# An attention and feed-forward kernel on one core: C v in 64x32 tiles, and another order of all steps

## The chip, the cores and the metric

The kernel runs on one core of a Trainium2 chip. The core has a matrix engine (TensorE, PE in the profile), three engines for vectors (VectorE = DVE, ScalarE = ACT, GpSimd = POOL), a sync engine (SP), and 16 DMA engines that all queues share. Each engine takes its own instructions strictly in the order in which they were written, and waits for the others by semaphores. The metric is the time of one execution in device microseconds (us), as the median of several runs.

## The reference

For 8 batches of 8 heads with 576 rows of 64 columns, the Nystroem form of attention, and behind it a feed-forward step on all 4608 tokens:

```
q_lm, k_lm = means of 18 rows each: 32 landmarks a head
A  = softmax(q k_lm^T / 8)        576 x 32
Bm = softmax(q_lm k_lm^T / 8)      32 x 32
C  = softmax(q_lm k^T / 8)         32 x 576
Z  = Bm^T / (|Bm|_1 |Bm|_inf);  six times  Z = 2 Z - Z Bm Z
x  = A Z C v                       576 x 64 a head, the 8 heads side by side: 4608 x 512
out = ((x w1) * (x w2)) w3 w_out   w1, w2: 512 x 1024, w3: 1024 x 1024, w_out: 1024 x 512
```

Inputs and outputs are fp32.

## The kernel before

The work is cut into steps, each the instructions of one engine, with a short name. A *quad* n (0 to 15) is four heads of one batch: batch b has the quads 2b and 2b+1. The kernel never forms x: it multiplies the small matrix W = Z C v (32 x 64 a head) by w1 and w2 first, and then A by the result.

- **Weights.** `w3n` loads w3 in eight chunks, four DMAs each on SP, `wf` loads w_out in four pieces, half on SP and half on ACT. DVE transposes a chunk (`tr`, L572), ACT and DVE split it and w_out into a high and a low fp16 half (`wh` L579, `wl` L587, `woh` L561, `wol` L566). PE multiplies chunk j with w_out in eight steps `mm{j}0` to `mm{j}7` of three products each, and ACT brings the result out (`wo`, L606). The outcome is w34 = w3 w_out in eight parts.
- **Quads.** `lq` loads k and q of a quad on POOL's queue, with a cast to fp16 (L651). DVE transposes them (`T`, L676). The means come from PE for the quads 0 and 1 (`mp`) and from POOL for the others (`ma` L684, `mb` L691); ACT scales them (`mk`). PE forms the scores of C (`S`, 32x32 tiles) and of A and Bm (`A`, whole array); maxima, exponentials, sums and norms follow on DVE, ACT and POOL (`sm`, `sw`, `sb`, `se`, `ct`, and `ar`, `am`, `as`, `ae`, `au`, `bo`, `an`, `aT`).
- **C v** (`C{b}`, `cv_mm`, L891). `lv` loads v on SP, four DMAs a quad. For each of nine chunks of 64 rows a product in a 64x64 tile takes two heads' columns of exp(C) against two heads' v: of the four blocks that this gives, the two with C and v of the same head count. A tenth product forms the sums with `unit64`. `co` (L909) divides by the sums on DVE.
- **Z.** For groups of one or two batches: `N` (norms), five rounds of `x` on PE and `y` on DVE, then `Z` and `zo`. All are fp32 products in 32x32 tiles.
- **W and U.** `W{b}` (`w_mm`) multiplies Z and C v, four products a batch; `wp` and `wq` split the result in two fp16 halves; `U` (64x32 tiles) multiplies by w1 and w2, and ACT brings U out (`uo`, L1035).
- **Dense work.** `d` multiplies U by A for both of w1 and w2, ACT copies one (`e`, L1110), DVE multiplies the two (`f`, L1116), `g` multiplies by w34, `h` (ACT, L1130) scales and `st` stores, two DMAs a tile of 128 tokens.

All matrix products are issued by the helper `mm`, so they have one line, L492; they are told apart by their tiles (xz is `x` and `Z`; vb,ecT is `C`; zb,cv is `W`; w,wT is `U`; aT,u is `d`; w,ab is `g`; wo,w3t is `mm`; bm is `N`). An fp32 product is issued as two matmuls with a weight load each.

**What sets the order.** A planner (`Plan.run`, L146) runs when the kernel is built. It keeps a ring of buffers for every kind of tile, and the eight PSUM banks as one ring. Step by step it takes, on the engine that can begin first, the ready step with the lowest entry in the table `PRIO`, with costs, DMA rates and instruction fetches that it assumes. The order that results is written out once and is fixed when the program runs. `GATE` holds loads back: the k and q of the quads 0 and 1 wait for `gw1`, a small POOL copy that reads w_out's second piece, and all later ones and the loads of w1 and w2 (`lw`, L669) wait for `gw3`, which reads its fourth. Eighteen products on a zeroed tile (`warm`, step `wu`) come first on PE.

Of the kernel before, what the change touches and what calls it, by code (L numbers as in the profile page):

```python
# [11 lines left out]
ALU = mybir.AluOpType  # L12
# [17 lines left out]
GATE = {**{n: ["gw3"] for n in range(2, 16)}, 0: ["gw1"], 1: ["gw1"], "w": ["gw3"]}  # L30
MEANPE = range(2)
WARM = 18
# [5 lines left out]

class Task:
    def __init__(self, name, eng, occ, fn, deps, acq, rel, anchor, off, kind, mode, lat, dma, n):  # L40
        self.name, self.eng, self.occ, self.fn, self.n = name, eng, occ, fn, n
        self.deps, self.acq, self.rel = deps, acq, rel
        self.anchor, self.off, self.kind = anchor, off, kind
        self.mode, self.lat, self.dma = mode, lat, dma
        self.prio = PRIO[name]
        self.ready = 0.0
        self.start = self.free = self.end = None


class Plan:  # L50
# [6 lines left out]

    LAT = {"PE": 0.2, "ACT": 0.15, "DVE": 0.13, "POOL": 0.1, "SP": 0.0}
    SELF = {"PE": 0.0, "ACT": 0.14, "DVE": 0.11, "POOL": 0.08, "SP": 0.0}
    NEAR = {"PE": 0.08, "ACT": 0.05, "DVE": 0.05, "POOL": 0.05, "SP": 0.0}  # L60
    SWITCH = 0.093
    BACK = 0.093
    FIRST, LAND = 1.3, 1.0
    PIECE, AHEAD, FETCH = 256, 60, 3.4
    STAY = 0.6
    RATE = {1: 0.88, 2: 1.08, 3: 1.08}
    BEGIN = {"PE": 1.0, "ACT": 0.7, "DVE": 0.8, "POOL": 1.2, "SP": 0.7}

    def __init__(self):
        self.tasks, self.by = [], {}  # L70
        self.rings, self.slot, self.left = {}, {}, {}
# [12 lines left out]
    def _slots(self, acq):  # L84
        got, when, taken = [], 0.0, set()
        for ring, key, uses in acq:
            free = self.rings[ring]
            some = [i for i, f in enumerate(free) if f is not None and (ring, i) not in taken]
            if not some:
                return None  # L90
            best = min(some, key=lambda i: (free[i], i))
            taken.add((ring, best))
            when = max(when, free[best])
            got.append((ring, key, best, uses))
        return when, got

    def _landed(self, limit):

        going, come = self.going, self.come
        while True:  # L100
            act = [q for q in QUEUES if going[q]]
            nxt = min([come[q][0][0] for q in QUEUES if come[q]], default=None)
            if not act and nxt is None:
                return None
            if not act:
                step = max(0.0, nxt - self.now)
            else:
                all_ = sum(going[q][0][1].dma[1] for q in act)
                rate = {q: self.RATE[len(act)] * going[q][0][1].dma[1] / all_ for q in act}
                step = min(going[q][0][0] / rate[q] for q in act)  # L110
                if nxt is not None:
                    step = min(step, max(0.0, nxt - self.now))
            if self.now + step > limit:
                step = limit - self.now
                if step <= 0.0:
                    return None
                for q in act:
                    going[q][0][0] -= step * rate[q]
                self.now = limit
                return None  # L120
            for q in act:
                going[q][0][0] -= step * rate[q]
            self.now += step
            for q in QUEUES:
                while come[q] and come[q][0][0] <= self.now + 1e-9:
                    t = come[q].pop(0)[1]
                    going[q].append([t.dma[0], t])
            for q in act:
                if going[q][0][0] <= 1e-9:
                    return going[q].pop(0)[1]  # L130

    def _finish(self, t):
        for key in t.rel:
            rec = self.left[key]
            rec[0] -= 1
            rec[1] = max(rec[1], t.end)
            if rec[0] == 0:
                self.rings[rec[2]][self.slot[key]] = rec[1]
        for u in self.after.get(t.name, ()):
            self.waiting[u.name] -= 1  # L140
            same = t.eng == u.eng and not t.dma
            u.ready = max(u.ready, t.free + self.SELF[t.eng] if same else t.end)
            if not self.waiting[u.name]:
                self.avail[u.eng].append(u)

    def run(self):  # L146
        free = dict(self.BEGIN)
        self.now, self.going, self.come = 0.0, {q: [] for q in QUEUES}, {q: [] for q in QUEUES}
        issued, landed = {q: 0 for q in QUEUES}, {q: [] for q in QUEUES}
        done, have, fetched = 0, [0.0, 0.0], 0.0  # L150
        mode = None
        self.waiting = {t.name: len(t.deps) for t in self.tasks}
        self.after, then = {}, {}
        for t in self.tasks:
            for d in t.deps:
                if d[0] == "~":
                    then.setdefault(d[1:], []).append(t)
                else:
                    self.after.setdefault(d, []).append(t)
        self.avail = avail = {e: [] for e in self.LAT}  # L160
        for t in self.tasks:
            if not self.waiting[t.name]:
                avail[t.eng].append(t)
        order, n = [], len(self.tasks)
        while len(order) < n:
            best = None
            for e, cand in avail.items():
                opts, first = [], None
                for t in cand:
                    at = max(free[e], t.ready)  # L170
                    if t.dma and issued[e] >= 8:
                        if len(landed[e]) <= issued[e] - 8:
                            continue
                        at = max(at, landed[e][issued[e] - 8])
                    if first is not None and at > first + self.NEAR[e]:
                        continue
                    got = ()
                    if t.acq:
                        found = self._slots(t.acq)
                        if found is None:  # L180
                            continue
                        at, got = max(at, found[0]), found[1]
                    if e == "PE" and mode is not None and t.mode != mode:
                        at += self.SWITCH if mode == "full" else self.BACK
                    opts.append((at, t, got))
                    if first is None or at < first:
                        first = at
                if not opts:
                    continue
                near = [o for o in opts if o[0] <= first + self.NEAR[e]]  # L190
                pick = min(near, key=lambda o: o[1].prio - (self.STAY if e == "PE" and o[1].mode == mode else 0.0))
                if best is None or pick[0] < best[0]:
                    best = pick
            t = self._landed(best[0] if best else 1e9)
            if t is not None:
                t.end = self.now + self.LAND
                landed[t.eng].append(t.end)
                self._finish(t)
                continue
            if best is None:  # L200
                left = [t.name for t in self.tasks if t.start is None]
                raise RuntimeError(f"stuck with {len(left)}: {left[:12]} {self.rings}")
            at, t, got = best
            e = t.eng
            avail[e].remove(t)
            t.start = at
            late = 0.0
            if e == "PE":
                mode = t.mode
                while (done + t.n + self.AHEAD) // self.PIECE >= len(have) - 1:  # L210
                    k = len(have) - 1
                    now = at + late + t.occ * max(0.0, self.PIECE * k - self.AHEAD - done) / t.n
                    late += max(0.0, have[k] - now)
                    fetched = max(fetched, now, have[k]) + self.FETCH
                    have.append(fetched)
                done += t.n
            t.free = free[e] = at + late + t.occ
            t.end = t.free + t.lat
            for ring, key, pick, uses in got:
                self.rings[ring][pick] = None  # L220
                self.slot[key] = pick
                self.left[key] = [uses, 0.0, ring]
            if t.dma:
# [1011 lines left out]
```

## Time and profile before

| | |
|---|---|
| median of 3 runs | 280.58 us (279.47 to 281.23) |
| the profiled execution | 280.17 us |
| its span, first to last instruction | 278.3 us |
| busy: PE | 257.2 us (92%) |
| busy: DVE | 194.0 us (70%) |
| busy: ACT | 164.0 us (59%) |
| busy: POOL | 132.3 us (48%) |
| mean granted clock of PE | 0.985 |
| HBM | 38.8 MB read, 9.4 MB written |

A busy share is a mean over the whole span. It says which engine has most to do, not what is late at a given place. Matmuls are pipelined, so a busy PE isn't one at its peak; small tiles run beside one another. The prediction therefore reads the busy times stretch by stretch, and the waits with their places. In the rows, "A <- B" at the end of a line tells what an engine waited for; "issue" is time in which it waited for nothing that the profile shows.

### The profile page before, as it was taken

How to read it: one execution, taken by the hardware profiler on the slowest of the kernel's cores; microseconds unless marked ns; L12 is line 12 of the kernel's file. 1: busy time of each engine (PE TensorE's matmuls, PEld its weight loads, DVE VectorE, ACT ScalarE, POOL GpSimd, SP SyncE). 2: the span in 40 equal slices, each digit the busy share in tenths (PEclk: the TensorE clock that was granted, in tenths of full speed). 3: DMA queues.
4: the chain of work that ended last, by engine and by line, in shares of the span. 5: the costliest groups of instructions: out<-in, count | busy, mean ns of one | idle time of the engine just before them, and what ended most of it. 6: DMA issues, size and time to landing. Idle time of an engine off the chain costs nothing.

```text
span 278.3 us, 9596 instructions
## 1 busy us (share of the span) xinstructions
PE 257.2 (92%) x3934; PEld 168.3 (60%) x3934; DVE 194.0 (70%) x470; ACT 164.0 (59%) x413; POOL 132.3 (48%) x147
## 2 busy tenths in 40 slices
PE   8668999989996699999999999899999999999993
PEld 2234344444693586667668777686687576864771
DVE  4669999999996499999999979674157153440440
ACT  0725565456446465999579543763645857648551
POOL 0362899999999398999997333003000000000000
PEclk9799999999999799999999999999999999999999
DMA  7999999999999426584958123502601043313334
GB/s 174 237 226 236 233 240 235 241 256 224 182 219 240 111 45 126 145 186 56 194 111 212 42 65 96 141 2 48 144 4 41 18 97 79 78 39 78 75 79 113
DMA packets 22509, 37.34 MB, mean 134 GB/s; under 512 B 3520, under 2 KB 7616, under 8 KB 22464
## 3 DMA queue, kind: packets, MB, share of 16 engines
q1 hardware_dynamic: 16128, 24.13, 35.5%
q0 software_dynamic: 5696, 11.54, 23.3%
q10 hardware_dynamic: 640, 1.05, 1.5%
q8 instruction: 31, 0.51, 0.8%
q14 instruction: 14, 0.11, 0.1%
HBM read 38.80 MB, written 9.44 MB: 173 GB/s over the span
## 4 chain that ended last, share of the span: by engine, by line
PE 58%; DMA 16%; POOL 10%; DVE 5%; issue 4%; ACT 4%; SPq 0%; ACTq 0%; POOLq 0%; DVEq 0%
PE bank L492 58%; DMA w3n<-in_moe_w_dram 5%; DMA nat<-in_k_dram 4%; POOL ls L691 4%; DMA ab<-in_moe_w_out_dram 3%; DMA vb<-in_v_dram 3%; POOL ls L684 3%; DMA u<-in_moe_w_out_dram 1%; POOL ah L825 1%; ACT lm L712 1%; POOL ea L797 1%; POOL nat L651 1%; DVE tiny L811 1%; DVE T L676 1%; DVE bank L572 1%
## 5 line engine op out<-in xcount | busy, mean ns | idle before, releaser
L1116 DVE TENSOR_TENSOR ab<-asb,bank 128x384 f16<-128x384 f16 x96 | 50.2, 547 | 41.1 <-ACT asb L1110 38.4
L492 PE MATMUL bank<-aT,u 128*128 128x192 f16 x768 | 70.0, 247 | 0.6 <-issue 0.5
L492 PEld LDWEIGHTS <-u 128*128 128x128 f16 x768 | 64.7, 99 | 7.4 <-issue 0.7
L492 PE MATMUL bank<-w,ab 128*128 128x512 f16 x288 | 67.3, 379 | 0.0
L1110 ACT CAST asb<-bank 128x384 f16<-128x384 f32 x96 | 45.2, 483 | 16.5 <-PE bank L492 13.2
L492 PE MATMUL bank<-wo,w3t 128*128 128x512 f16 x192 | 47.0, 388 | 3.5 <-ACT wo L561 2.2
L492 PEld LDWEIGHTS <-ab 128*128 128x128 f16 x288 | 27.2, 98 | 28.6 <-issue 1.4
L691 POOL TENSOR_TENSOR ls<-ls 128x128 f32<-128x128 f32 (+2 forms) x56 | 40.8, 729 | 3.4
L1130 ACT ACTIVATE osb<-bank 128x512 f32<-128x512 f32 x36 | 21.5, 602 | 32.4 <-PE bank L492 31.9
L1035 ACT CAST u<-bank 128x512 f16<-128x512 f32 x64 | 33.0, 616 | 5.9 <-PE bank L492 5.9
L825 POOL TENSOR_TENSOR ah<-ea,tiny 128x576 f16<-128x576 f32 x16 | 18.5, 1162 | 33.3 <-DVE aT L834 32.8
L684 POOL TENSOR_TENSOR ls<-nat 128x1152 f32<-128x1152 f16 x14 | 33.2, 2375 | 2.3 <-ACT lm L712 1.6
L492 PEld LDWEIGHTS <-w3t 128*128 128x128 f16 x192 | 18.3, 101 | 26.2 <-issue 4.9
L676 DVE STREAM_TRANSPOSE T<-nat 128x576 f32<-128x576 f32 x32 | 24.1, 755 | 2.3 <-DMA nat<-in_q_dram 1.6
L492 PE MATMUL bank<-T 32*32 32x288 f16 (+1 forms) x320 | 19.0, 293 | 4.3 <-issue 2.2
L797 POOL TENSOR_TENSOR ea<-ea,tiny 128x608 f32<-128x608 f32 x16 | 19.4, 1214 | 3.1 <-DVE tiny L791 3.1
L492 PE MATMUL bank<-xz 32*32 32x64 f32 (+1 forms) x768 | 17.0, 215 | 2.8 <-issue 2.6
L761 ACT ACTIVATE ec<-bank,tiny 128x288 f32<-128x288 f32 x32 | 16.0, 504 | 5.1 <-DVE tiny L753 5.0
L492 PE MATMUL bank<-vb,ecT 64*64 64x128 f32 x576 | 18.5, 272 | 0.2 <-issue 0.2
L492 PEld LDWEIGHTS bank<-xz 32*32 32x32 f32 x768 | 13.1, 105 | 9.0 <-issue 4.8
L492 PE MATMUL bank<-w,wT 64*32 64x512 f16 x512 | 17.3, 378 | 1.1 <-ACT ec L761 1.1
L492 PEld LDWEIGHTS bank<-vb,ecT 64*64 64x64 f32 x576 | 16.6, 133 | 1.7 <-issue 0.9
(76 smaller groups left out, 292.5 us busy)
## 6 DMA issues: line engine op xcount, KB each, us to landing
vb<-in_v_dram SPq DMA_DIRECT2D x64, 144.0 KB, 4.7
out_dram<-osb SPq DMA_DIRECT2D x72, 128.0 KB, 2.4
nat<-in_k_dram POOLq DMA_DIRECT2D x16, 288.0 KB, 7.4
nat<-in_q_dram POOLq DMA_DIRECT2D x16, 288.0 KB, 7.9
w3n<-in_moe_w_dram SPq DMA_DIRECT2D x32, 128.0 KB, 12.2
w<-in_moe_w_dram POOLq DMA_DIRECT2D x4, 512.0 KB, 16.2
u<-in_moe_w_out_dram ACTq DMA_DIRECT2D x4, 128.0 KB, 4.5
ab<-in_moe_w_out_dram ACTq DMA_DIRECT2D x4, 128.0 KB, 4.1
```

The source lines that it names most:

```text
L492: nc.tensor.matmul(out_, lhsT, rhs, start=start, stop=stop, **({} if pos is None else {"tile_position": pos}))
L572: nc.vector.transpose(out=bank(at(f"w3f{j}{h}")).rearrange("p (e g i) -> p g e i", e=4, g=4), in_=w3n[at(f"w3n{j}")].rearrange("p g (e x) ...
L676: nc.vector.transpose(out=Ts[at(f"T{n}")][:, GRP * t:GRP * t + GRP] .rearrange("p r l e -> p (r l e)").bitcast(FP32), in_=nats[at(f"nat{n} ...
L684: nc.gpsimd.tensor_tensor(out=l, in0=nat[:, :, 0:9, :], in1=nat[:, :, 9:18, :], op=ALU.add)
L691: nc.gpsimd.tensor_tensor(out=l[:, :, x:x + m, :], in0=l[:, :, x:x + m, :], in1=l[:, :, y:y + m, :], op=ALU.add)
L761: nc.scalar.activation(out=ecs[at(f"ec{n}")][:, hp, :], in_=two(f"pS{n}")[hp][:, 0:288], func=AXF.Exp, scale=SCALE, bias=t[:, 2 + hp:3 + h ...
L797: nc.gpsimd.tensor_tensor(out=ea, in0=ea, in1=tinies[at(f"ta{n}")][:, 0:19].unsqueeze(2).to_broadcast([128, 19, M]), op=ALU.subtract)
L825: nc.gpsimd.tensor_tensor(out=ahs[at(f"ah{n}")].rearrange("p g m r -> p g r m"), in0=eas[at(f"ea{n}")][:, 0:GRP, :].rearrange("p (g r) m - ...
L1035: nc.scalar.copy(out=uu[at(f"u{b}{qd}")][:, wi, 512 * half:512 * half + 512], in_=bank(at(f"pU{b}{wi}{half}{qd}")))
L1110: nc.scalar.copy(out=asb[at(f"as{b}{j}{ch}")], in_=d1_ps(b, j, ch)[0])
L1116: nc.vector.tensor_mul(abts[at(f"ab{i // 2}")][:, 2 * j:2 * j + 2, CH * (i % 2):CH * (i % 2) + CH], asb[at(f"as{b}{j}{ch}")], d1_ps(b, j, ...
L1130: nc.scalar.activation(out=osb[at(f"os{i}")], in_=bank(at(f"pE{i}")), func=AXF.Copy, scale=2.0 ** -12)
```

## The change

- **C v, each head by itself.** The products go from 64x64 to 64x32 tiles: 32 columns of one head's exp(C) against that head's 64 columns of v. There are eight products a chunk instead of four, half as wide. A batch is cut in two steps, `C{b}a` (chunks 0 to 4) and `C{b}` (chunks 5 to 8 and the sums), which may have other steps between them.
- **W in two products.** C v now stands with one head in each 32 rows, so `W` takes two products of 128 columns instead of four of 64, and `co` handles half the columns.
- **The first q and k aren't gated.** The quads 0 and 1 load without `gw1`. The first w3 chunk is loaded by SP and ACT, two DMAs each, ahead of w_out on both.
- **Warm-up** is four steps of six products, which the order places.
- **The order is given.** `PRIO` and the planner's run are gone. A list `ORDER` names every step in order, with the buffers that it takes. Each engine's steps keep the order in which the list names them.
- **The last tile** (tile 35) is formed in two halves of 256 columns, each with its own scaling and two stores, one of them on ACT's queue.

The diff, cut. The whole list `ORDER` has some 70 lines; its first lines, and those around the first dense steps, are shown.

```diff
-GATE = {**{n: ["gw3"] for n in range(2, 16)}, 0: ["gw1"], 1: ["gw1"], "w": ["gw3"]}
+GATE = {**{n: ["gw3"] for n in range(3, 16)}, 0: [], 1: [], 2: ["gw3"], "w": ["gw3"]}
-WARM = 18
+WARM = 6
+ORDER = """
+w3n0a.0 w3n0.0:0 ca w3n0a w3n0 cb lq00:0 wf0a.0 cc wf0s.0 wf0a wf0s lq01 wf1a.0 wf1s.0 lq10:1 wf1a wf1s lq11
+wf2a.0 wf2s.0 wf2s wf3s.0 tr00:0.0 wf3s zz wh00 tr01:1 wu1:2 w3n1.0:1 wh01 wu0:3 T00:0 woh0 gw0 w3n1.1 wl01 wf2a
+wl00 wu3:4 woh1 wol0 wf3a.0 w3n1.2 wf3a mm00:5 T01 mp0:6 woh2 gw1 w3n1 wol1 woh3 wol2 mm01 mk0:0 wol3 w3n2.0:2
+lt0 T10:1 A0:7.2 woh5 gw2 w3n2.1 mm02 ar0:0 woh4 S0:1.3 wol5 mm03 am0:0 w3n2.2 wol4 mp1:0 sm0:1 woh6 gw3 w3n2
+lq20:2 woh7 w3n3.0:0 T11 mm04 as0 mk1:1 w3n3.1 wol6 mm05 w3n3.2 lq21 wol7 sw0 ae0 w3n3 mm06 lq30:3 sb0 tr10:4.1
...
+S6:2.3 aT4:4 U010:7.1 am6:1 N1:6.3 uo0101 sm6:7 uo0100 mm76 se50:1 T80:0 sw6 lq101 mm77 se51 bt1 T81 as6 C1a:1.7
+mk7:1 sb6 no1:0 d000:4.5 an5:0 C1 lt7 e000:0 ct5:1 ma8:0 se60:0 aT5:5 d011:6.4 wo7 lv6.0:2 f000:0 se61 lv6.1
...
     def run(self):
...
+        order = []
+        for word in ORDER.split():
+            name, _, slots = word.partition(":")
+            t = self.by[name]
+            for (_, key, _), x in zip(t.acq, slots.split(".") if slots else ()):
+                self.slot[key] = int(x)
+            order.append(t)
...
-    def load_w3(j):
-        def fn(a):
-            nc.sync.dma_start(
+    def load_w3(j, eng, a0):
+        def fn(x):
+            a = a0 + x
+            eng.dma_start(
...
-                        r, o = slice(64 * (h2 ^ qd), 64 * (h2 ^ qd) + 64), 64 * h2
-                        if c < NC9:
-                            mm(ps[qd][o:o + 64, 0:128],
-                               ecTs[at(f"ecT{n}")][r, c, :, :].rearrange("p a m -> p (a m)"),
-                               vbs[at(f"vb{n}")][r, :, c, :],
-                               start=(c == 0), stop=(c == NC9 - 1), pos=(r.start, o))
+                        r = slice(64 * (h2 ^ qd), 64 * (h2 ^ qd) + 64)
+                        for a in range(2):
+                            o = 64 * h2 + 32 * a
+                            if c < NC9:
+                                mm(ps[qd][o:o + 32, 0:D], ecTs[at(f"ecT{n}")][r, c, a, :], vbs[at(f"vb{n}")][r, a, c, :],
+                                   start=(c == 0), stop=(c == NC9 - 1), pos=(r.start, o))
...
-            for x in range(2):
-                for s in range(2):
-                    zb = zbs[at(f"zb{i}")][:, 2 * b - 2 * GROUPS[i][0] + s, :, :]
-                    mm(ps[64 * s:64 * s + 64, 0:128].rearrange("p (e a m) -> p a e m", e=2, a=2)[:, x], cvs[at(f"cv{b}")][:, s, x, :],
-                       zb.rearrange("p (e a) m -> p a e m", a=2)[:, x], pos=(0, 64 * s))
+            for s in range(2):
+                mm(ps[64 * s:64 * s + 64, 0:128], cvs[at(f"cv{b}")][:, s, :],
+                   zbs[at(f"zb{i}")][:, 2 * b - 2 * GROUPS[i][0] + s, :, :].rearrange("p h m -> p (h m)"), pos=(0, 64 * s))
...
-        add(f"C{b}", "PE", 2.2, cv_mm(b), deps=[f"ct{n0}", f"ct{n1}", f"lv{n0}", f"lv{n1}", "cc"],
-            acq=both(f"pC{b}", 1),
+        cvd = [f"ct{n0}", f"ct{n1}", f"lv{n0}", f"lv{n1}", "cc"]
+        add(f"C{b}a", "PE", 0.85, cv_mm(b, 0, 5), deps=cvd, acq=both(f"pC{b}", 1),
+            rel=[f"ecT{n0}", f"ecT{n1}", f"vb{n0}", f"vb{n1}", f"mx{n0}", f"mx{n1}"],
+            at=(p, 2.0), mode="64x32", kind="C", n=160)
+        add(f"C{b}", "PE", 0.85, cv_mm(b, 5, 10), deps=[f"C{b}a"],
...
+            for c in range(8):
+                mm(ps[:, 0:256], ab[:, c, 256:384], w34[:, c, 256 * h:256 * h + 256], start=(c == 0), stop=(c == 7))
```

More of the change, by code (lines that the diff above doesn't have):

```diff
@@ L82, in add @@
         return t
[L84 to L144, printed above, removed]
@@ L146, in run @@
-    def run(self):
[L147 to L223, printed above, removed]
-                issued[e] += 1
-                self.come[e].append((t.free + self.FIRST, t))
-                for u in then.get(t.name, ()):
-                    self.waiting[u.name] -= 1
-                    u.ready = max(u.ready, t.free)
-                    if not self.waiting[u.name]:
-                        avail[e].append(u)
-            else:
-                self._finish(t)
-            order.append(t)
-        while True:
-            t = self._landed(1e9)
-            if t is None:
-                return order
-            t.end = self.now + self.LAND
```

205 lines of the change are left out of this document (146 added, 59 removed), and 166 rows, old and new, of the table PRIO.

## The prediction

> **What bounds the kernel now.** I read the busy time in stretches of 10 us first, then PE's waits, then the chain in order of time. (Columns of the stretches: length, busy us of PE, PEld, DVE, ACT, POOL, granted clock, DMA share, GB/s.)
>
> ```profile
> 0.00:10.00 10.00, 7.02 (x18) 2.45 (x18) 4.24 (x28) 1.87 (x3) 0.68 (x6) 1.00 0.82 197
> 10.00:20.00 10.00, 6.66 (x21) 2.34 (x21) 7.14 (x11) 4.99 (x10) 6.50 (x12) 0.83 1.08 225
> 20.00:30.00 10.00, 8.91 (x86) 5.30 (x87) 9.99 (x20) 4.41 (x15) 3.44 (x5) 1.00 1.12 235
> ...
> 80.00:90.00 10.00, 7.64 (x254) 5.38 (x253) 7.16 (x27) 5.64 (x17) 9.58 (x12) 1.00 1.03 233
> 90.00:100.00 10.00, 7.39 (x103) 6.45 (x104) 6.07 (x16) 6.08 (x19) 5.00 (x4) 0.83 0.42 90
> ...
> 270.00:280.00 10.00, 3.82 (x18) 1.56 (x16) 0.00 (x0) 1.79 (x3) 0.00 (x0) 0.85 0.34 79
> sum 280.00, PE 257.22 PEld 168.30 DVE 194.00 ACT 164.05 POOL 132.35; mean PE 9.19 PEld 6.01 DVE 6.93 ACT 5.86 POOL 4.73
> ```
>
> PE bounds it: 257.2 of 278.3 us busy. The 21.1 idle us are 7.4 in the first 30 (2.98, 3.34, 1.09), 5.0 between 80 and 100, 4.5 behind the last product, and 4.2 in all the rest. Two of these stretches also have a clock of 0.83, that is some 3.4 us at half speed, which loses 1.7 us each. So an edit pays if it takes work from PE or closes one of the two holes. The holes near 85 and 92:
>
> ```profile
> PE bank L492 <- issue: 5.9, 5, 2.6
> ...
> 84.16 2.15 issue
> 86.31 3.67 PE bank L492 x128
> 89.98 2.63 issue
> ...
> 203.12 0.51 issue
> ...
> q8 instruction: 31, 0.51, 0.8%
> ```
>
> PE waits here for no engine. The first row is PE's waits, the next ones the chain, the last one the DMA queues. PE's 7868 instructions (counted in the program) came in 31 transfers, so about 256 each, and between the two stops lie 128 products with 128 weight loads: exactly one piece. I read this as PE running out of instructions. At 86 to 92.6 a piece took 3.67 + 2.63 = 6.3 us to come, at a DMA share of 1.0; at 203 the 128 products ahead of the stop reach back to about 200.7, so there it took 2.9.
>
> **The change, part by part.** *C v.* One batch now, then what a product costs in other tiles:
>
> ```profile
> 111.22 2.19 PE L492 MATMUL bank<-vb,ecT 64*64 64x128 f32 x72
> 113.24 0.24 PE L492 MATMUL bank<-tiny,unit 64*64 64x2 f32 x8
> 113.41 0.45 PE L492 MATMUL bank<-T 32*32 32x288 f16 x16
> ...
> 121.18 0.44 PE L492 MATMUL bank<-bm 32*32 32x32 f32 x30
> ...
> 88.11 0.65 PE L492 MATMUL bank<-xz 32*32 32x64 f32 x32
> 88.69 0.94 PE L492 MATMUL bank<-w,wT 64*32 64x512 f16 x16
> ...
> L492 PE MATMUL bank<-bm 32*32 32x32 f32 x128 | 2.2, 192 | 0.3 <-issue 0.3
> L492 PE MATMUL bank<-wo,w3t 128*128 128x512 f16 x192 | 47.0, 388 | 3.5 <-ACT wo L561 2.2
> ```
>
> 80 records take 113.41 - 111.22 = 2.19 us, 27 ns each. They become 160 of half the columns in eight tiles instead of four. If columns alone count, that is half, 1.09. If starts count: 30 starts of 32 columns took 0.44 - 0.19 = 0.25, 8.3 ns each, so 1.33; and 64 fp32 columns on four tiles (32 records in 88.69 - 88.11, less 0.14 for the change of tiling below) took 14 ns, so 2.2, no gain. I take 1.33, the row where no tile is waited for twice: 8 x (2.19 - 1.33) = **-6.8** (bounds -8.8 and 0).
>
> *Changes of tiling.* In the two instruction orders PE changes its tiling 81 times before and 122 after: C v is cut in two with dense work between, and small steps are mixed more finely with dense ones.
>
> ```profile
> 49.36 2.75 PE L492 MATMUL bank<-wo,w3t 128*128 128x512 f16 x12
> 52.04 0.43 PE L492 MATMUL bank<-xz 32*32 32x64 f32 x16
> 52.40 0.93 PE L492 MATMUL bank<-wo,w3t 128*128 128x512 f16 x3
> ```
>
> Twelve products last 2.75, so with the 388 ns of one they start 0.215 apart and end their turn after 2.58; the next step starts after 2.68: 0.10 for going in. The 16 of xz take 0.36 to the next start, and another 16 (0.58 above) 0.22 more, so 0.14 for coming out. Mean 0.115: 41 x 0.115 = **+4.7** (bounds 4.1 and 5.7).
>
> *W and its scaling.* Two products of 128 columns for four of 64 stream as much, and the smaller DVE work behind C v (0.1 us a batch) runs where DVE is off the path: 0. The last tile cut in halves is no longer last in the new order, so the end (last product to the end of the span, 4.4 us) stays: 0.
>
> *The start.* The first rows of the time line:
>
> ```profile
> 1.36 7.02 PE L492 MATMUL bank<-aT 128*128 128x512 f16 x18 [1.36 <-DVE aT L510]
> 7.81 1.32 DVE L572 STREAM_TRANSPOSE bank<-w3n 128x512 f32<-128x512 f32 x2 [3.73 <-DMA u<-in_moe_w_out_dram]
> 10.58 0.40 PE L492 MATMUL bank<-wo,w3t 128*128 128x512 f16 x1 [2.20 <-ACT wo L561]
> 11.92 0.72 POOL L651 DMA_DIRECT2D nat<-in_k_dram  x1
> 14.20 0.83 POOL L612 COPY gates<-ab 128x1 f32<-128x1 f32 x2
> 17.65 0.78 DVE L676 STREAM_TRANSPOSE T<-nat 128x576 f32<-128x576 f32 x1 [0.74 <-DMA nat<-in_k_dram]
> 20.00 0.78 DVE L676 STREAM_TRANSPOSE T<-nat 128x576 f32<-128x576 f32 x1 [1.58 <-DMA nat<-in_q_dram]
> 20.71 1.28 DVE L572 STREAM_TRANSPOSE bank<-w3n 128x512 f32<-128x512 f32 x2
> 31.28 0.61 PE L492 MATMUL bank<-wo,w3t 128*128 128x512 f16 x2
> ```
>
> Now k and q are issued at 11.92, behind W_out's gate, and k is used 5.7 us later, q 2.35 after that. After, they are issued behind POOL's first constant, at about 1.4, next to two other queues, so I put the four loads at 8, 11, 14.5 and 17.5 (about 3.2 apart, not 2.35). DMA runs at 0.82 in the first 10 us and 1.08 behind them, so there is room for hardly 3 us of transfers: what k and q gain, W_out loses, and its last piece moves from 14.2 to about 18. The first w3 chunk, at the head of two queues, comes at about 6.2 instead of 7.8. DVE is in order: w3 transpose, then the memset that the warm-up products wait for, then the transpose of k (8.1), and only then the halves of w3 and W_out. So warming starts at 7.2 instead of 1.4. Its first 18 products took 7.0, mostly at half speed; I take 5.8, as the clock rises by the middle: first real product at 13.0 instead of 10.6. From 6.2 on DVE has 22 steps until the transpose of the second w3 chunk: four of q/k and eight of W_out by the rows below, ten smaller ones, 14.5 us by their durations and some 13.5 as they overlap (two transposes take 1.32 in a row above). With waits of some 2.9 for W_out and the mean that transpose comes at 22.6 instead of 20.7, but with 4.3 us of q/k work done that came later before. Down to the first product of the third w3 chunk (31.28 now) this makes 32.3: **+1.0** (bounds: -2 if DVE never waits, +3 if the warm-up is cold throughout, 18 x 0.43 = 7.7). The new order holds one more warm-up group in front of the second q/k; that is in it.
>
> ```profile
> L676 DVE STREAM_TRANSPOSE T<-nat 128x576 f32<-128x576 f32 x32 | 24.1, 755 | 2.3 <-DMA nat<-in_q_dram 1.6 <-DMA nat<-in_k_dram 0.7
> L566 DVE SCALAR_TENSOR_TENSOR wo<-u,wo 128x512 f16<-128x512 f32 x4 | 2.6, 686 | 0.0
> ```
>
> *Instructions.* 9112 instead of 7868, 36 pieces. C v is now 320 instructions in about 1.6 us, cut so that a piece's border falls inside. The holes of today close, because the dense work of batch 0 moves between C 0, C 1 and C 2: 2.15 + 2.63 + 1.7 of half speed = **-6.5**. In their place, adding up PE's work piece by piece with the durations above, the shortest pieces after hold 2.7, 2.8 (C 1, C 2), then 2.8, 2.9, 3.6 and 3.8 us. At 2.9 us a fetch they stop PE for 0.4 in all, at 6.3 the two around C 1 and C 2 and the 4.3 between them for 9.1. By then fewer loads are queued than at 84 now, so I take 4.2 there and 2.9 behind: 1.5 + 1.4 + 0.3 = **+3.2** (bounds 0.4 and 9.1).
>
> *The rest.* Two queues are passed. On SP the first two v loads now go between the w3 chunks 4 to 7; those chunks are used later and among dense work, so 0. On POOL the four W1/W2 loads move behind more q/k work:
>
> ```profile
> L684 POOL TENSOR_TENSOR ls<-nat 128x1152 f32<-128x1152 f16 x14 | 33.2, 2375 | 2.3 <-ACT lm L712 1.6 <-issue 0.7
> L691 POOL TENSOR_TENSOR ls<-ls 128x128 f32<-128x128 f32 (+2 forms) x56 | 40.8, 729 | 3.4
> L797 POOL TENSOR_TENSOR ea<-ea,tiny 128x608 f32<-128x608 f32 x16 | 19.4, 1214 | 3.1 <-DVE tiny L791 3.1
> w<-in_moe_w_dram POOLq DMA_DIRECT2D x4, 512.0 KB, 16.2
> ```
>
> Ahead of the last one POOL has four means (2.4 + 40.8/14 = 5.3 each), seven steps of 1.2, and twenty issues of 0.6, some 40 us, most of it behind 18: it is issued near 57 and lands between 65 and 73, where the first U product wants it at about 69 (12 us of PE work ahead of the first dense one). I take 0; late, it holds PE up to 3. The 4.2 idle us elsewhere I leave (DVE is as full as now until the dense work): 0 (bounds -2 and +3, W1/W2 in it).
>
> Sum: -6.8 + 4.7 + 1.0 - 6.5 + 3.2 = -4.4, so the span 278.3 becomes 273.9. The profiled run was 280.17, 1.9 above its span, and close to the median 280.58: **275.8**.
>
> A page of the Trainium skill speaks against the change. "TensorE: Matmul & The Clock Gate", section "Wait — 56ns, not 53.3ns?", says that matmul starts never come closer than about 25 ns, however narrow; by it C v would take 160 x 25 = 4.0 us a batch, and the time would be some 297. The row of bm, 30 starts in 0.25 us, does not agree: beside one another in small tiles they start at 8.3.
>
> **The rivals.**
> 1. *All covers hold.* C v at 1.09, fetches at 2.9 everywhere, DVE never late: -2.0, -2.8, -3.0, so 268. For it: the order leaves no piece under 2.7 us. Against: DMA at 1.03 in 80 to 90.
> 2. *Instructions bind, slower than before.* Place: C 1 and C 2 with the first dense work. If DMA is as full there as now, 6.3 us a piece gives 9.1 for 3.0, and half speed returns behind such a stop (1.7): 275.8 + 7.8 = 283.6. It decides from about 5.5 us a piece, where the loss (8.0) eats the gain. For it: two of the five stops now lie there. Against: part of the loads are through by then.
> 3. *C v isn't faster* (14 ns a record, as xz): +6.8, so 282.6. For it: xz has the same 64 fp32 columns. Against: xz uses four tiles, C v eight.
> 4. *A start costs what it costs now*, 27 ns: 160 x 27 = 4.3 us a batch instead of 1.33, +24, so 300. Against it: bm's row. The rule of the Trainium skill cited above is of this kind.
> 5. *A load comes late in an in-order queue.* DVE stands at k's transpose if that load lands at 11 instead of 8, or PE at the first U product for W2: +3 to +5, so 280.
>
> **How the numbers follow.** Forecast 0.45 (272 to 279), rival 1 0.2, rival 2 0.15, rival 3 0.1, rival 5 0.07, rival 4 0.03. A measurement here tells some 1%, 2.8 us. Faster: rival 1 and four fifths of the forecast, 0.57; slower: rivals 2, 4 and a little of 3, 0.2; the rest 0.23. The range of 8 in 10 goes from rival 1 to rival 2 with a margin: 267 to 285.
>
> **What would show it.** C v: 160 records a batch in 1.3 to 1.6 us. PE's waits on issue: 3 to 4 us, under 2 each, none followed by half speed. The first real product near 13, the third w3 chunk near 32. The first dense product, now in the row below, near 82. Wrong it would be if DVE or PE stand for a load before 30 us by more than 3, or if C v costs 2 us or more.
>
> ```profile
> 93.58 1.44 PE L492 MATMUL bank<-aT,u 128*128 128x192 f16 x8
> ```

## The result, and the profile after

| | before | after |
|---|---|---|
| median of 20 runs each | 278.48 us (275.68 to 282.62) | 281.38 us (278.46 to 284.39) |
| profiled run, its span | 280.17, 278.3 us | 282.35, 280.6 us |
| ratio, 95% interval | | 1.0105 (1.0081 to 1.0129) |

The kernel became 1.05% slower, where 1.7% faster was predicted; 281.38 lies inside the range of 267 to 285, but on the other side of the kernel before. Span against span it is +2.3 us instead of -4.4. Some executions of every kernel here fall into a slower state: the ratios, here and below, compare only the others, while the medians are over all.

The changed kernel in stretches of 10 us, with the columns of the prediction's table (the last row adds up thirty stretches, the last of them empty):

```profile
60.00:70.00 10.00, 7.81 (x69) 3.49 (x68) 9.93 (x25) 6.00 (x17) 9.89 (x11) 1.00 1.11 242
70.00:80.00 10.00, 9.72 (x81) 3.75 (x80) 6.45 (x15) 5.37 (x14) 8.03 (x9) 0.83 1.09 229
...
90.00:100.00 10.00, 8.06 (x260) 6.97 (x250) 7.58 (x21) 4.36 (x13) 9.61 (x11) 0.83 0.76 156
...
sum 300.00, PE 255.43 PEld 163.78 DVE 192.06 ACT 161.81 POOL 132.04; mean PE 8.51 PEld 5.46 DVE 6.40 ACT 5.39 POOL 4.40
```

PE is busy for 255.4 us instead of 257.2, so the work itself hardly shrank, and it stands idle for 25 us instead of 21. The holes of before at 84 and 92 are smaller, but there is a new one between 60 and 70, and the clock of 0.83 is back twice. What PE waits for names the pieces:

```profile
PE bank L243 <- DVE aT L261: 6.6, 1, 6.6
PE bank L243 <- issue: 6.1, 5, 1.9
PE bank L243 <- DMA w<-in_moe_w_dram: 2.5, 1, 2.5
```

The first row is the start, before the warm-up begins. The pieces of the chain:

```profile
59.34 10.89 DMA w<-in_moe_w_dram
...
91.58 1.94 issue
...
113.98 0.57 issue
...
159.32 1.39 issue
...
180.17 1.64 issue
...
205.25 0.58 issue
```

There are 6.1 us of waits on issue, which I read as stops on instructions, against 5.9 before; they did not go, they moved and spread along the kernel, to 205. And the last of the four W1/W2 loads, issued at 59.34, takes 10.89 us to land, with PE standing in front of it at the second U step of batch 0, the first that uses it. Single steps in the time line of PE:

```profile
6.57 6.79 PE L243 MATMUL bank<-aT 128*128 128x512 f16 x18 [6.57 <-DVE aT L261]
13.20 0.89 PE L243 MATMUL bank<-wo,w3t 128*128 128x512 f16 x3
...
32.07 2.10 PE L243 MATMUL bank<-wo,w3t 128*128 128x512 f16 x9
...
70.28 1.05 PE L243 MATMUL bank<-w,wT 64*32 64x512 f16 x16 [2.47 <-DMA w<-in_moe_w_dram]
71.26 2.59 PE L243 MATMUL bank<-wo,w3t 128*128 128x512 f16 x6
...
83.14 1.04 PE L243 MATMUL bank<-vb,ecT 64*32 64x64 f32 x80
84.10 0.83 PE L243 MATMUL bank<-aT,u 128*128 128x192 f16 x8
84.87 0.80 PE L243 MATMUL bank<-vb,ecT 64*32 64x64 f32 x60
...
87.40 0.70 PE L243 MATMUL bank<-T 128*128 128x320 f16 x4 [0.81 <-ACT ea L559]
87.94 1.48 PE L243 MATMUL bank<-aT,u 128*128 128x192 f16 x16
89.35 0.48 PE L243 MATMUL bank<-xz 32*32 32x64 f32 x20
...
93.51 1.29 PE L243 MATMUL bank<-vb,ecT 64*32 64x64 f32 x90 [1.94 <-issue]
...
94.89 2.72 PE L243 MATMUL bank<-aT,u 128*128 128x192 f16 x16
...
142.68 1.66 PE L243 MATMUL bank<-vb,ecT 64*32 64x64 f32 x140
...
144.42 0.82 PE L243 MATMUL bank<-T 32*32 32x288 f16 x18
```

To read in them: C v of one batch, undisturbed, takes 144.42 - 142.68 = 1.74 us for its 160 records, 10.9 ns each (the 140 of the first row and 20 that follow it singly). The first real product starts at 13.20. The first dense product starts at 84.10 instead of 93.58 (near 82 was predicted). Behind the wait of 2.47 six products take 2.59 us, behind the stop at 91.58 sixteen dense ones take 2.72, both at a lowered clock.

### The profile page after: what moved, and what is told of

Read it like the earlier page. It is cut to its first block, busy times and chain, and to the rows that moved or that the text cites. A ratio compares the mean times of both kernels' runs of the same rounds, so it can differ in the third digit from the quotient of the medians.

```text
span 280.6 us, 10784 instructions
## 1 busy us (share of the span) xinstructions
PE 255.4 (91%) x4556; PEld 163.8 (58%) x4556; DVE 192.1 (68%) x470; ACT 161.8 (58%) x414; POOL 132.0 (47%) x147
## 4 chain that ended last, share of the span: by engine, by line
PE 67%; DMA 13%; POOL 7%; issue 4%; ACT 4%; DVE 3%; ACTq 0%; SPq 0%; POOLq 0%; DVEq 0%
PE bank L243 67%; DMA w<-in_moe_w_dram 4%; POOL ls L445 3%; DMA u<-in_moe_w_out_dram 3%; DMA nat<-in_q_dram 3%; DMA ab<-in_moe_w_out_dram 3%; POOL ls L438 3%; ACT lm L466 1%; DVE T L430 1%; DMA w3n<-in_moe_w_dram 1%; ACT u L786 1%; DVE tiny L565 1%; POOL w L423 0%; ACT ec L515 0%; POOL nat L405 0%
## 5 line engine op out<-in xcount | busy, mean ns | idle before, releaser
L870 DVE TENSOR_TENSOR ab<-asb,bank 128x384 f16<-128x384 f16 x96 | 49.2, 543 | 39.4 <-ACT asb L864 38.1
L243 PE MATMUL bank<-aT,u 128*128 128x192 f16 x768 | 71.8, 249 | 2.2 <-issue 2.2
L243 PE MATMUL bank<-w,ab 128*128 128x512 f16 (+1 forms) x296 | 68.5, 374 | 2.0 <-issue 2.0
L864 ACT CAST asb<-bank 128x384 f16<-128x384 f32 x96 | 44.5, 487 | 26.5 <-PE bank L243 22.9
L786 ACT CAST u<-bank 128x512 f16<-128x512 f32 x64 | 34.9, 604 | 11.8 <-PE bank L243 10.3
L884 ACT ACTIVATE osb<-bank 128x512 f32<-128x512 f32 x35 | 20.6, 602 | 31.3 <-PE bank L243 31.1
L243 PE MATMUL bank<-w,wT 64*32 64x512 f16 x512 | 18.7, 387 | 2.6 <-DMA w<-in_moe_w_dram 2.5
L243 PE MATMUL bank<-vb,ecT 64*32 64x64 f32 x1152 | 15.0, 228 | 1.9 <-issue 1.9
L243 PEld LDWEIGHTS bank<-vb,ecT 64*32 64x32 f32 x1152 | 13.1, 106 | 4.8 <-issue 3.4
```

The source lines that it names most:

```text
L243: nc.tensor.matmul(out_, lhsT, rhs, start=start, stop=stop, **({} if pos is None else {"tile_position": pos}))
L786: nc.scalar.copy(out=uu[at(f"u{b}{qd}")][:, wi, 512 * half:512 * half + 512], in_=bank(at(f"pU{b}{wi}{half}{qd}")))
L864: nc.scalar.copy(out=asb[at(f"as{b}{j}{ch}")], in_=d1_ps(b, j, ch)[0])
L870: nc.vector.tensor_mul(abts[at(f"ab{i // 2}")][:, 2 * j:2 * j + 2, CH * (i % 2):CH * (i % 2) + CH], asb[at(f"as{b}{j}{ch}")], d1_ps(b, j, ...
L884: nc.scalar.activation(out=osb[at(f"os{i}")], in_=bank(at(f"pE{i}")), func=AXF.Copy, scale=2.0 ** -12)
```

## The experiments

Two theories were tried. **Theory A**: the W1/W2 loads come late because POOL issues them late, which costs the 2.5 us and the half speed behind them. **Theory B**: the new form of C v has twice as many instructions, and PE, which takes them in pieces of 256, stops for them. Their rivals stand in each expectation.

### The form of C v and the order, each alone

The change has two large parts: how C v is computed, and the order with its early q and k. The first pair exchanges them. The changed order with the old form:

```
-                        for a in range(2):
-                            o = 64 * h2 + 32 * a
-                            mm(ps[qd][o:o + 32, 0:D], ecTs[..][r, c, a, :], vbs[..][r, a, c, :], ...)
+                        mm(ps[qd][o:o + 64, 0:128], ecTs[..][r, c, :, :].rearrange(...), vbs[..][r, :, c, :], ...)
```

and W in four products with it; the cut into chunks 0 to 4 and 5 to 9 stays.

> The changed kernel's order with the products of before: C v in 64x64 tiles (half as many instructions, still in two parts a batch) and W in four products. Theory B (C v's extra instructions make the stops on instructions): of 6.1 us of issue waits at most 2 stay, the half speed behind them goes, C v costs 0.45 us a batch more (2.2 against 1.75): 281.4 - 5.5 + 3.6 = 279.5, ratio 1.003. Rival (the stops come from where the dense work stands, not from C v's number): the stops stay, 285, ratio 1.023.

The old order with the new form is the same edit the other way round, in the kernel before, with C v in one piece a batch:

> The kernel before, in its own order, with the new C v (64x32 tiles, in one piece a batch) and W in two products. C v 2.2 to 2.45 us a batch becomes 1.75 if a record costs the 10.9 ns seen in the changed kernel. Theory B: the two holes at 84 and 92 grow by 0.5 to 2 us each and new ones open behind, so that of -4 in C v at most 1 us is left: ratio 0.996 to 1.004. Rival (the instructions are hidden by the products): the whole 4 us show, ratio 0.986.

| | old order | new order |
|---|---|---|
| old C v | before, 1 | 0.9806 (0.9725 to 0.9887) |
| new C v | 1.0589 (1.0492 to 1.0686) | after, 1.0105 (1.0081 to 1.0129) |

The new form costs 16 us in the old order and about 8 in the new one; the new order gains with either form, and the change as made is the sum of a loss of about 3% and a gain of about 2%. The old form in the new order took 273.7 us, less than theory B (279.5) or its rival (285) had expected. Its waits of PE have no row of issue at all; these are the largest:

```profile
PE bank L243 <- DVE aT L261: 6.6, 1, 6.6
PE bank L243 <- DMA w<-in_moe_w_dram: 0.8, 1, 0.8
```

So the stops went, as theory B has it. The wait for the load shrank too, from 2.5 to 0.8, which neither theory had; that the form does this is not shown (the next two runs of this version show 1.9 and 0.8). And the dense products behind C v of batch 2 run at full speed:

```profile
88.81 1.49 PE L243 MATMUL bank<-aT,u 128*128 128x192 f16 x16
```

The instruction queue of this run, on the page's list of DMA queues, then the same row of the changed kernel:

```profile
q8 instruction: 31, 0.51, 0.8%
```

```profile
q8 instruction: 35, 0.57, 0.9%
```

The new form in the old order (296.06 us) is the opposite: its chain is cut by stops all along. Theory B had expected a ratio of 0.996 to 1.004 and its rival 0.986, so the direction is theory B's, and the size is far from both.

```profile
71.73 3.00 issue
...
81.32 2.73 issue
...
177.72 1.90 issue
179.62 1.82 PE bank L492 x87
181.44 2.85 issue
184.28 8.80 PE bank L492 x234
```

PE waits 18.5 us for issue there, in 8 stops. Between 179.62, where one piece had come, and 184.28, where the next had, lie 252 products and weight loads by the trace's records: one piece. So it took 4.66 us to come, at a DMA share of 0.46 in the stretch from 180 to 190, while PE needed 1.82 us for what it had. The clock falls with it; two stretches of the same run:

```profile
170.00:180.00 10.00, 8.09 (x340) 5.75 (x337) 8.07 (x19) 3.70 (x9) 4.75 (x4) 1.00 0.36 84
180.00:190.00 10.00, 7.15 (x266) 5.21 (x270) 4.07 (x15) 2.95 (x7) 0.00 (x0) 0.61 0.46 123
```

That the changed order holds its advantage with the old form was measured twice more, the second time in more rounds:

> The order of the changed kernel with the old form of C v once more, beside the others on one chip. Its first profile showed a wait of 0.8 us at the first U product where all other runs of this order showed 2.1 to 3.7. If that was chance, the profile now shows about 2 and the ratio is nearer 0.985 than 0.981; if the old form makes it, it shows 0.8 again.

276.7 us, ratio 0.981 (0.9664 to 0.9955); its profile, of an execution of 277.71 us where the fastest took 273.54, shows 1.9 us at the load and one stop of 1.3 on instructions at C 2, so neither is fixed by the form alone.

> The order of the changed kernel with the old form of C v, a third time and in more rounds, as the version that beats both: theory B gives 7 us less than the changed kernel (stops 6.1 and their half speed 1.5 to 2.4 gone, C v 3.4 more, the rest by the load at the first U product): ratio 0.978 to 0.988.

276.48 us, ratio 0.9876 (0.9798 to 0.9953), and in its profile no stop on instructions and 0.8 us at the load. The three ratios lie between 0.981 and 0.988 (by the medians over all runs, 0.979 to 0.992): this version beats both kernels. Theory B's 7 us less than the changed kernel came out as 8.3 in the first run and 6.4 in the third, by the ratios.

### Is it PE's work, or its instructions?

Half the columns in each product of C v in the changed kernel:

```
-mm(ps[qd][o:o + 32, 0:D], ecTs[..][r, c, a, :], vbs[..][r, a, c, :], ...)
+mm(ps[qd][o:o + 32, 0:32], ecTs[..][r, c, a, :], vbs[..][r, a, c, 0:32], ...)
```

> The changed kernel with half the columns of v in every product of C v (32 instead of 64; the other half of C v is filled with a copy, so this part of the computation is left out). If the columns set a record's 10.9 ns, C v falls from 1.75 to about 1 us a batch, if the start of a product or its weight load does, it stays at 1.6 to 1.75. Either way theory B says that the time stays within 1.5 us of the changed kernel (280 to 282.5), since the pieces around C v then wait for instructions instead; the rival (PE's work sets the time there) gives 275.

280.26 us, ratio 1.0041 (1.0002 to 1.0081). C v of batch 4 in its time line, first to next step:

```profile
141.53 1.47 PE L243 MATMUL bank<-vb,ecT 64*32 64x32 f32 x142
...
143.06 0.70 PE L243 MATMUL bank<-T 32*32 32x288 f16 x17
```

1.53 us for 160 records, 9.6 ns each instead of 10.9: half the columns took away an eighth of the time. So columns make little of this price; most of it comes with each record, a product with its weight load. PE waits 6.6 us for issue here, against 6.1. Whether the 8 x 0.21 = 1.7 us that PE saved are lost to the stops, as theory B has it, can't be told: the total fell by 1.1 us by the medians and 1.8 by the ratios. The rival's 275 did not come, but neither did the C v of about 1 us that it needs.

### The same number of instructions in other places

The new order, with the new form in four batches only. By the borders of the pieces in the trace of the old form, batches 0, 3, 4 and 5 lie in pieces that hold more PE work, 1, 2, 6 and 7 in short ones.

```
+NARROW = (0, 3, 4, 5)      # the other run: (1, 2, 6, 7)
+    def cv_mm(b, c0, c1):
+        return (cv_mm_32 if b in NARROW else cv_mm_64)(b, c0, c1)
```

> The order of the changed kernel, C v in the new form for batches 0, 3, 4 and 5 and in the old form (64x64 tiles, half the instructions) for 1, 2, 6 and 7. Theory B: a piece of 256 instructions takes 3 to 4.7 us to come in the quiet stretches and up to 6.3 where the DMA engines are full, so a batch gains where its pieces hold more PE work than that. By the borders counted in the run with the old form these four batches do: 4 x 0.42 = 1.7 us off that run and no stop on instructions over 0.6: 273.7 - 1.7 = 272, ratio to before 0.974. Rival (any narrow batch brings its share of stops, half of the 7.7 us): 277.5, ratio 0.993.

> The same with the forms exchanged: the new form in batches 1, 2, 6 and 7, as many instructions and as much PE work saved as in the run with 0, 3, 4 and 5. Theory B: here two halves of C v or C v and Z fall into pieces with 2 to 3 us of PE work; stops of some 4 to 5 us in all (at C 1, C 2 and C 6) for 1.7 saved: 273.7 + 3 = 277, ratio 0.991, 4 to 5 us above the run with 0, 3, 4 and 5. Rival (only the number of instructions counts): both runs alike within 1 us.

275.17 us against 279.96; ratios 0.9877 (0.9814 to 0.994) and 1.0049 (1.002 to 1.0079), so 4.8 us apart with the same number of instructions (33 transfers of the instruction queue in both) and the same work. The second one's chain around C 2, and the dense products behind it:

```profile
89.68 3.15 issue
92.83 24.67 PE bank L244 x443
```

```profile
93.41 2.74 PE L244 MATMUL bank<-aT,u 128*128 128x192 f16 x16
```

The first one's waits of PE have no row of issue. The stop of 3.15 and the 1.25 that those sixteen products lose against 1.49 make 4.4 of the 4.8 us between the two. That confirms the place; the rival (both alike within 1 us) is out. The levels came out wrong: theory B expected 272 and 277, both runs took 3 us more, and only one of the three stops expected for the second came. Of the 1.7 us that the new form should save in the four quiet batches nothing is seen (275.17 against 273.7 to 276.7 for the old form).

The cut in two parts, undone: the first half of C 0, C 1, C 3 and C 5 moves right in front of the second, as in the other four already (the list moves all eight, but only in these four did PE have another step between).

```
-... C1a:1.7 mk7:1 sb6 no1:0 d000:4.5 an5:0 C1 ...
+... mk7:1 sb6 no1:0 d000:4.5 an5:0 C1a:1.7 C1 ...
```

> The changed kernel with the first half of each C v moved right ahead of the second (batches 0, 1, 3 and 5, the other four are so already). By the prediction's price of a change of tiling 4 x 0.23 = 0.9 us less PE work; by theory B the 320 instructions in 1.75 us add 1 to 3 us of stops at C 1, C 3 and C 5: 281.4 + 1 = 282.5, ratio 1.014. Rival (the cut is worth nothing): 280.5, ratio 1.007.

285.75 us, ratio 1.0234 (1.0169 to 1.0299). The new largest stop stands where the 160 records of C 5 now follow one another:

```profile
157.19 2.35 issue
159.54 23.75 PE bank L239 x560
```

That is slower than theory B's 1.014 as well. The stops add up to 7.0 instead of 6.1, and the wait for W1/W2 is 3.7 in this run instead of 2.5; the latter is a part of the 3.6 us between the two kernels that the place of C v does not explain, and the rest was not followed. So the cut pays for its changes of tiling, but how much of it by fewer stops is not shown.

### The late load

> The changed kernel with the two late W1/W2 loads taken ahead of the q/k load of the seventh quad on POOL's queue, nothing else moved. Theory A (POOL's order makes them late): they are issued near 43 instead of 55.6 and 59.3, land before 62, the first U product no longer waits (2.65 us) and the half speed behind it (1.6 us) goes: about 4 us off, 277.2, ratio to before 0.995. Rival (the DMA engines are full until 77 us, so what W1/W2 gain the q/k and v loads behind them lose): another wait of 2 to 4 us turns up between 45 and 70, and the ratio stays at 1.005 to 1.012.

```
-... mm27 y0_1:2 lq60:2 ... lw00 ... lw01 ...
+... mm27 y0_1:2 lw00 lw01 lq60:2 ...
```

284.09 us, ratio 1.0194 (1.0109 to 1.0279): slower rather than faster than the changed kernel, though the two intervals touch. The load is on time, and another is late:

```profile
PE bank L239 <- DMA vb<-in_v_dram: 3.7, 1, 3.7
```

The v of batch 0 now arrives 3.7 us after C v wants it, the other wait that the rival expected. Theory A fell in this form. A smaller move, to 52.6:

> The changed kernel with its two late W1/W2 loads one step earlier on POOL's queue, ahead of the second load of the seventh quad (near 52.6 instead of 55.6 and 59.3); the run that took them at 43 pushed a v load behind them. Theory A (the loads are late because POOL issues them late, and between 52 and 67 there is room): the first U product waits under 0.7 instead of 2.65 and the half speed behind it goes, C v of batch 0 waits under 0.5: 281.4 - 3.5 = 278, ratio 0.998. Rival (the DMA engines carry all they can until 77, any order leaves a load late): ratio 1.006 to 1.012, with a wait of 2 us or more at C 0, U 0 or a q/k load.

282.36 us, ratio 1.0061 (1.0025 to 1.0097), against 1.0105: by the ratios some 1.2 us gained where 3.5 were expected, with intervals that overlap. PE waits for no load any more, but now 1.36 us inside the fourth U step of batch 0, by this chain:

```profile
75.04 2.38 POOL ls L434
77.42 1.12 POOL ah L575
...
79.01 0.45 DVE ea L535
...
79.50 4.23 PE bank L239 x129
```

POOL's mean comes first, then its scaling (ah), which gives back the buffer that DVE's transpose (ea) needs, and that transpose empties the bank that PE wants. With the load on time POOL ends last; in the changed kernel it is busy for 9.89 of the 10 us between 60 and 70, in the row above. A second, longer wait is now in front of the scores of A:

```profile
87.66 0.70 PE L239 MATMUL bank<-T 128*128 128x320 f16 x4 [1.95 <-ACT asb L860]
88.19 2.10 PE L239 MATMUL bank<-aT,u 128*128 128x192 f16 x16
```

In the changed kernel PE waits 0.81 there (the row of 87.40). Behind the 1.95 sixteen dense products take 2.10 instead of 1.48, so the half speed did not go either, it moved. The move in the other two versions:

> The same move in the order with the old form of C v. Theory A: a wait of 0.8 to 2.2 us at the first U product goes: 1 to 3 us under the run of the old form without the move, about 272. Rival: no gain, 274.

> The same move with the new form of C v in batches 0, 3, 4 and 5 only. Theory A: its wait of 2.2 us at the first U product and 1.3 of half speed behind it go: 275.2 - 3.5 = 271.7. Theory B: 4 x 0.42 = 1.7 us under the run with the old form and the same move, if no new stop on instructions appears. Rival: 275.

276.97 us, 0.9874 (0.977 to 0.9978), and 275.45 us, 0.9863 (0.9755 to 0.9972): no gain that can be told apart from the versions without the move, where theory A expected 272 and 271.7. The second once more:

> The new form of C v in batches 0, 3, 4 and 5 alone, and the late W1/W2 loads near 52.6, in more rounds. If C v's 1.7 us show where no piece is short, the ratio is 0.005 or more below that of the old form beside it; if DVE and ACT take over as the bound around the first U product and C v's 1.7 us are lost to their waits, the two are alike within 0.003.

276.38 us, 0.9932 (0.9895 to 0.9969), beside 0.9876 for the old form (without the move of the load): not 0.005 below it but as much above, with intervals that overlap. Its profile doesn't show the case that was meant, though:

```profile
96.30 0.43 PE L240 MATMUL bank<-xz 32*32 32x64 f32 x8 [1.76 <-issue]
96.66 1.46 PE L240 MATMUL bank<-aT,u 128*128 128x192 f16 x8
```

PE stops there for 1.76 us with half speed behind (eight dense products in 1.46, as long as sixteen take elsewhere), where the profile of the same kernel in the run before has no row of issue. So a stop comes in one execution of a kernel and not in another, and what the new form is worth where no piece is short stays open; no gain from it was seen.

### The early q and k alone

```
+    early = [P.by[x] for x in ("lq00", "lq01", "lq10", "lq11")]
+    order = [t for t in order if t not in early]
+    x = order.index(P.by["cb"]) + 1
+    order[x:x] = early
```

> The kernel before with the q/k loads of the first two quads right behind POOL's first constants, ahead of W_out's gate; every other instruction stays where it was. By the prediction's start (a wash): the loads land 5 us earlier, W_out's last pieces some 3 later, the third w3 chunk within 1 us of 31.3, ratio 0.997 to 1.004. Rival (the start waits for q and k): the chunk comes 3 us earlier, ratio 0.99.

283.29 us, ratio 1.0145 (1.0065 to 1.0226). Neither side was right: the start got slower.

```profile
11.32 1.32 DVE L572 STREAM_TRANSPOSE bank<-w3n 128x512 f32<-128x512 f32 x2 [7.18 <-DMA w3n<-in_moe_w_dram]
...
14.84 2.59 PE L492 MATMUL bank<-wo,w3t 128*128 128x512 f16 x5 [7.90 <-ACT wo L561]
...
36.58 0.61 PE L492 MATMUL bank<-wo,w3t 128*128 128x512 f16 x2
```

The first w3 chunk is transposed at 11.32 instead of 7.81 and the first real product moves from 10.58 to 14.84, since that chunk and W_out's pieces come later; the row of 36.58 is the third w3 chunk, 5.3 us behind the 31.28 of before. In an order that was not made for it, the early q and k take the DMA engines from w3 and W_out.

## Why the prediction was wrong

- **C v, -6.8: mis-sized.** From 2.19 to 1.74 us, 8 x 0.45 = -3.6. A record of 64 fp32 columns in a 64x32 tile takes 10.9 ns, between the 8.3 of bm's row that I took and the 14 of xz's that I kept as the other end; the 9.6 ns with half the columns show that columns make little of it. The rule of the Trainium skill, page "TensorE: Matmul & The Clock Gate", section "Wait — 56ns, not 53.3ns?", no start closer than about 25 ns, does not agree with this trace either: starts lie 10.9 ns apart. Rival 4 is out.
- **Changes of tiling, +4.7: right in size.** The first half of C 1 takes 0.96 to the dense products behind it (83.14 to 84.10), against 0.87 for half of the undisturbed 1.74: 0.09 for coming out of the small tiles. Eight dense products take 0.77 to the small ones behind them (84.10 to 84.87), sixteen take 1.41 (87.94 to 89.35), so eight alone cost 0.64 and going in 0.13. The mean is 0.11, and 41 changes make 4.5.
- **W, its scaling, the end: 0, right within 0.5.** The last product ends 4.9 us ahead of the span's end instead of 4.4.
- **The start, +1.0: right within 0.5.** The first real product came at 13.20 (13.0 predicted), but partly by luck: the warm-up began earlier (6.57, not 7.2) and lasted longer (6.6 to the next product, not 5.8). The third w3 chunk starts three products behind 32.07, at about 32.7 (32.3). The runs add that the same early loads cost 5 us there in the old order; that they gain anything in the new one is not shown.
- **The old holes, -6.5: right for themselves.** Both closed as the dense work moved, and in the new order with the old form two profiles of three show no stop at all, the third one of 1.3. Those holes alone are about as much as that version gains in its first run (a span of 272.1 against 278.3).
- **The new stops, +3.2: the step that failed.** They take 6.1, with half speed behind the one at 91.58 (sixteen dense products in 2.72 where the old form's run has them in 1.49), and a clock of 0.83 over 10 us is 3.4 us at half speed, a loss of at most 1.7: together about 7.5. What I had wrong is the time that a piece takes to come. The 2.9 us, which I took for everything behind C 2, were read from one stop of before, by counting back over its 128 products only; counted in records of products and weight loads from one border to the next, the same piece takes 3.4, and the stops after C 2 end 3.2 (114.6), 4.5 (160.7), 4.2 (181.8) and 3.6 (205.8) us behind the border before them. At C 2 it is at least 93.51 - 87.40 = 6.1, not 4.2 (7.2 if the border lies a few records earlier, in front of the wait that ends at 87.40). It is no fixed time: a piece of some 2.5 us passed without a stop in the first run of the old form, one of 3.2 in the kernel before. With 4 us for a quiet piece the prediction's own list of short pieces (2.8, 2.9, 3.6 and 3.8) would have given 2.9 there instead of 0.3 (by that list at 2.9 us it is only 0.1), without half speed. "None followed by half speed" was wrong as well.
- **W1/W2 behind q and k, 0: wrong, its bound of +3 too small.** The wait is 2.47, and the products behind it lose some 1.7 more (six in 2.59 instead of 0.38 + 5 x 0.215 = 1.46, and sixteen of U, 0.98 to the next step instead of 0.44 where they run undisturbed). But an earlier place does not give it back: the experiments turn it into a late v load, or into a wait that ends with POOL's mean.
- **What I left at 0 elsewhere** hides a gain. The terms as measured (-3.6, +4.5, +1.5, -6.5, about +7.5, +4) add up to some 7 where the span shows 2.3; some 5 us less were lost elsewhere. PE's idle time behind 30 us, without the waits on issue, the load and the end, shrinks only from 3.3 to 2.7 us, so most of the 5 lies in time that counts as busy. No run tests that; it stays open which part of the order does it.
- **All together.** The stops came out 4.3 above their term, the load 4 and C v 3.2; these three turned a gain of 4.4 into a loss, and the open 5 us made the loss smaller than it would have been.

Rival 2 comes nearest to what happened: instructions bind, half speed returns, with 283.6 forecast for 282.35 in the profiled run. That this number is near is luck: of its price only part arose at C 2 and none at C 1, and the rest at stops that I had written off and at the load. Rival 5's second half, a load late at U, came true beside it (at the second U step, which is the first to use it), and rival 3 is half true. I had given the three 0.32 together; they are not exclusive, as their shares supposed: each took its part of one sum.

The Trainium skill, page "Runtime: NRT & Kernel Launch", section "Instruction fetch mechanics", says that instructions are refilled in blocks of 256, fetched by the sequencer's own DMA while the block before runs. The traces agree: counted in PE's records, the five stops of the changed kernel end at record 2225, 3245, 5541, 6561 and 7581, so 1020, 2296, 1020 and 1020 apart, which is 4, 9, 4 and 4 times 255; and the instruction queue made 31, 33 and 35 transfers for 7868, 8504 and 9112 of them. It says too that crossing a border is mostly hidden; that does not hold here, where PE uses up a block of small products in 1.8 us (the row of 179.62) and then stands for 2.85.

## What to carry to other kernels

In 64x32 tiles a product and its weight load are two instructions that PE ran in 10.9 ns here: 256 instructions last 1.4 us, and the next 256 took 3.2 to 6.3 us to come. So before products are cut into more and smaller ones, add up PE's time from one border of 256 instructions to the next; where it is under the longest fetch seen, not the shortest, the cut can buy waiting. And a load that PE waited for while the DMA engines were full was not mended here by issuing it earlier: look first at which load it pushes back, and which engine ends last once it is on time.

## What was not expected of the hardware

- In 64x32 tiles one record of an fp32 product, with its weight load, costs 9.6 ns with 32 columns and 10.9 with 64: the price is nearly one per record, not per column.
- A piece of 256 instructions took 4.66 us to come where the DMA engines were at 0.46, and PE's clock in that stretch was 0.61; eight stops in that run made 18.5 us of waiting, and it took 16 us more than the kernel before although C v's own products had become cheaper.
- The stops can be moved by place alone: 4.8 us between two kernels with equal work and equal numbers of instructions. And one kernel (the new form in four batches, with the loads near 52.6) showed no stop in one profile and one of 1.76 us in another.
